# A drain of GpSimd between the scatters of the last wide item and the last block, in a fused attention and mixture-of-experts kernel

## The chip, the cores and the metric

The kernel runs on one core of a Trainium2 chip. The metric is the device time of one execution in microseconds (us), as a median over several runs. The profile is of one further execution.

## The reference

The reference computes a clustered attention and feeds its output, one row of 512 numbers per token, to a router with eight experts. Cut to what matters:

```python
# attention: 4 batches, 8 heads, 768 positions, head size 64, 16 clusters per head
mask = q_assign[:, :, :, None] == k_assign[:, :, None, :]     # nearest centroid of q and of k
scores = np.where(mask, scale * q @ k.T, -1e9)
attn = softmax(scores) @ v
x = attn.transpose(0, 2, 1, 3).reshape(3072, 512)

# router: 3072 tokens, 8 experts, hidden size 1024
expert_idx = argmax(cosine(x, expert_emb) / tau)
for e in range(8):
    mask = expert_idx == e
    out[mask] = gate_w[mask, None] * (np.maximum(x[mask] @ w1[e], 0) @ w2[e])
```

Every token goes to one expert alone, so the rows of x have to be gathered by expert, and the results scattered back to the rows of the output.

## The kernel before

The kernel has two phases. In the first (up to about 340 us) it works through 16 pairs of heads: TensorE makes the scores, ScalarE the exponentials, TensorE the product with v, and the finished rows go to a buffer x_rows in HBM. In the second, the tokens are sorted by expert, and the two matrix products of each expert are done in "items": four early blocks of 128 rows, then eight wide ("sized") items, one per expert, of 272 down to 160 rows, between single blocks of 128 rows. The list of kinds is at line 1314; it ends with a wide item and a block. The order of all instructions on all five engines is the order of the program's text (tc.manual_schedule, line 1404); no scheduler moves them, and each engine takes its own instructions in that order.

GpSimd issues all the indirect transfers of the second phase. gather (line 1038) fetches 128 rows, or quarter rows of 128 numbers, by an index per partition; scatter (line 1048) writes such rows to the output. A wide item's result is scattered by send (line 1238), one scatter for each 32 rows of it: nine for the widest, five for the last. A block's result (result, line 1268) is scaled by ScalarE with the gate and scattered at once by one scatter of 128 whole rows (line 1287). Both are recorded at line 1050. No engine waits for a scatter but to use its buffer anew, and at the end, where the output has to be complete.

The loop over the later items (line 1558) works one item ahead. For item i it does, in this order: the transposition of the next item's rows, the fetch of the one after it, send of the wide item before it (line 1570), the first matrix product of item i (hidden or sized_hidden), the loads of further weights, and the second product (result or sized_result). In the last round (i == LAST) item i is the last block: so its scatters on GpSimd are the five of the last wide item, from send at line 1570, and then the one of the block, from result. Two rounds from the end (line 1560) stands overflow(), a branch that does more blocks if an expert got more tokens than its places hold. In the profiled execution GpSimd skips it.

Behind the program's last statement (all instructions of it are recorded at the last line of the launch, L1634) each engine has a drain and then a barrier. An engine reports to GpSimd that it has come, and waits until GpSimd lets all go. SyncE first waits for every transfer to have landed. GpSimd has one drain before the barrier. After the barrier it clears the semaphores, with two more drains, and a second barrier ends the program. With the one at the program's start GpSimd has four drains.

Of the kernel before, what the change touches and what calls it, by code (L numbers as in the profile page):

```python
# [39 lines left out]
def kernel(  # L40
# [12 lines left out]
    nc = tc.nc  # L53
# [994 lines left out]
    def scatter(to, at, of, n):  # L1048

        inst = nc.gpsimd.indirect_dma_start(  # L1050
            out=to,
            out_offset=bass.IndirectOffsetOnAxis(ap=at, axis=0),
            in_=of,
            in_offset=None,
            bounds_check=n - 1,
            oob_is_err=False,
        ).ins
        tc.declare_no_dep(
            inst, group="out", reason="a row of out is written by one slot of one item"
        )  # L1060
        tc.add_to_no_dep_group("out", inst)
# [16 lines left out]
    def weights1(it, parts=1):  # L1078
        it.e = expert_of(it)
        for i in range(parts):  # L1080
            load_part(w1s[it.slot], moe_w1, it.e, KD, i, parts)

    def weights2(it, parts=1):
        for i in range(parts):
            load_part(w2s[it.slot], moe_w2, it.e, KF, i, parts)
# [7 lines left out]
    def fetch(it):  # L1093
        mo[it] = {}
        if it.kind == "sized":
            u0, n = FIRST[it.j], WIDE[it.j]
            xs = mo[it]["xs"] = szp.tile([P, max(WIDE), P], F32, tag="xs", name="xs")
            for u in range(n):
                gather(xs[:, u], x_pieces, flat(gpidx)[:, u0 + u : u0 + u + 1], NQ * N)
            return  # L1100
        if it.kind == "whole":
            xin = mo[it]["xin"] = it.xin
            gather(
                xin.rearrange("p w x -> p (w x)"), x_rows, it.tables[1][:, it.col : it.col + 1], N
            )
            return
        xin = mo[it]["xin"] = xip.tile([P, NQ, P], F32, tag="xin", name="xin")
        if it.kind == "early":
            n = SA * P
            gather(  # L1110
                xin.rearrange("p w x -> p (w x)"), x_rows[0:n], gidxs[0][:, it.j : it.j + 1], n
            )
            return
        for w in range(NQ):
            gather(xin[:, w], x_pieces, it.tables[0][:, it.col, w : w + 1], NQ * N)
# [11 lines left out]
    def turn_x(it, evict=None, xT=None):  # L1127
        d = mo[it]
        if it.kind == "sized":
            n = WIDE[it.j]  # L1130
            d["xT"] = szp.tile([P, KD, SQ * max(WIDE)], F32, tag="xTs", name="xTs")
            for u in range(0, n, NQ):
                m = min(NQ, n - u)
                nc.vector.transpose(
                    d["xT"][:, :, SQ * u : SQ * u + SQ * m].rearrange(
                        "p c (w t) -> p w c t", t=SQ
                    ),
                    d["xs"][:, u : u + m].rearrange("p w (c i) -> p w c i", i=SQ),
                )
            return  # L1140
        d["xT"] = mop.tile([P, DM], F32, tag="xTm", name="xTm") if xT is None else xT
        if it.kind == "block":
            nc.vector.transpose(
                d["xT"].rearrange("p (c w t) -> p w c t", c=KD, t=SQ),
                d["xin"].rearrange("p w (c i) -> p w c i", i=SQ),
            )
            return
        bk = psX.tile([P, DM], F32, tag="x_ps", name="x_ps")
        for c in range(KD):
            nc.tensor.transpose(  # L1150
                bk[:, P * c : P * c + P], d["rows"][:, c].rearrange("p w i -> p (w i)"), ident
            )
        evict(d["xT"], bk)

    def order_w2(it):

        w2 = mo[it]["w2"] = szp.tile([P, KF, DM], F32, tag="w2o", name="w2o", bufs=1)
        for f in range(KF):
            nc.vector.tensor_copy(
                w2[:, f].rearrange("p (g w i) -> p g w i", w=NQ, i=SQ),  # L1160
                w2s[it.slot][:, f].rearrange("p (w g i) -> p g w i", w=NQ, i=SQ),
            )
# [75 lines left out]
    def send(it):  # L1238

        u0 = FIRST[it.j]  # L1240
        for u in range(WIDE[it.j]):
            at = flat(spidx)[:, u0 + u : u0 + u + 1]
            scatter(out_pieces, at, mo[it]["ys"][:, u], NQ * N)
        del mo[it]

    def flat(t):
        return t.rearrange("p k w -> p (k w)")
# [156 lines left out]
    with tc.manual_schedule(engines=by_hand):  # L1404
# [118 lines left out]
        def overflow():  # L1523
            n_used = nc.values_load(used[0:1, 0:1], min_val=0, max_val=KX + NO)
            slot = later[-1].slot

            def more(j0, n):
                for j in range(j0, j0 + n):
                    it = Item("whole", KX + j, slot, more_tables)
                    it.col, it.gates, it.xin = j, more_gates, xin  # L1530
                    weights1(it)
                    weights2(it)
                    fetch(it)
                    order_x(it)
                    turn_x(it, nc.scalar.copy)
                    hidden(it)
                    result(it)

            with tc.If(n_used > KX):  # L1539
                more_tables = [None] + [  # L1540
                    mop.tile([P, NO], I32, tag=f"more{i}", name=f"more{i}", bufs=1)
                    for i in range(2)
                ]
                xin = szp.tile([P, max(WIDE), P], F32, tag="ys", name="ys")[:, 0:NQ]
                pb.hot_blocks(NB, NO)
                pb.tokens(NO)
                pb.token_rows(more_tables[1], more_tables[2])
                more_gates = mop.tile([P, NO], F32, tag="more_gates", name="more_gates", bufs=1)
                pb.hot_gates(NO)
                pb.gates(more_gates)  # L1550
                more(0, MORE[0])
                with tc.If(n_used > KX + MORE[0]):
                    more(MORE[0], MORE[1])
                    with tc.If(n_used > KX + MORE[0] + MORE[1]):
                        more(MORE[0] + MORE[1], MORE[2])

        LAST = len(later) - 1
        for i, it in enumerate(later):
            if i == LAST - 1:
                overflow()  # L1560
                weights1(later[LAST])
                weights2(later[LAST])
            if it.kind == "sized":
                order_w2(it)
            if i + 1 < len(later):
                turn_x(later[i + 1])
            if i > 0 and i + 2 < len(later) and later[i + 2].kind == "sized":
                fetch(later[i + 2])
            if i > 0 and later[i - 1].kind == "sized":
                send(later[i - 1])  # L1570
            if it.kind == "sized":
                sized_hidden(it)
            else:
                hidden(it)
            if i == 0:
                pb.gates(slot_gates)
            for j in range(i + 2, min(i + 4, len(later))):
                if later[j].kind == "block" and later[j] not in mo:
                    if it.kind == "sized":
                        nc.gpsimd.tensor_copy(pace, mo[it]["hT"][0:1, KF - 1, 0:1])  # L1580
                        fetch(later[j])
            if i + 2 < LAST:
                weights1(later[i + 2])
                if it.kind == "sized":
                    weights2(later[i + 2])
            if it.kind == "sized":
                sized_result(it)
            else:
                result(it)
            if i == 0:  # L1590
                fetch(later[2])
            if i + 2 < LAST and it.kind != "sized":
                weights2(later[i + 2])
# [45 lines left out]
```

## Time and profile before

| What | Value |
|---|---|
| Median of 6 runs | 712.4 us (710.99 to 713.04) |
| The profiled execution: its own time | 713.68 us |
| Its span, first to last instruction | 711.8 us |
| Busy share of the span: TensorE, VectorE, ScalarE, GpSimd | 98%, 54%, 38%, 38% |
| Granted TensorE clock, mean | 0.993 |
| Scatters of the output, from wide items and from blocks | 56 and 12 |
| Gathers | 96, of which 56 for wide items |
| Landing of a scatter of a wide item, median from its issue | 2.4 us |

The profile's page gives for each engine the busy time, then the chain of waits followed back from the last instruction, and the costliest groups of instructions. Register, branch and semaphore instructions and drains are not counted as busy; a q behind an engine's name (POOLq, SPq) marks the work of its sequencer, such as waits and drains. POOL is GpSimd, PE TensorE, DVE VectorE, ACT ScalarE, SP SyncE. In the timeline each line has the start and the length in us, then engine, line, operation, output and input, and in brackets the idle time before it and what ended it. The length of an indirect transfer's record is what GpSimd spends on it and not the time until its data has landed.

### The profile page before, as it was taken

How to read it: one execution, taken by the hardware profiler on the slowest of the kernel's cores; microseconds unless marked ns; L12 is line 12 of the kernel's file. 1: busy time of each engine (PE TensorE's matmuls, PEld its weight loads, DVE VectorE, ACT ScalarE, POOL GpSimd, SP SyncE). 2: the span in 40 equal slices, each digit the busy share in tenths (PEclk: the TensorE clock that was granted, in tenths of full speed). 3: DMA queues.
4: the chain of work that ended last, by engine and by line, in shares of the span. 5: the costliest groups of instructions: out<-in, count | busy, mean ns of one | idle time of the engine just before them, and what ended most of it. 6: DMA issues, size and time to landing. Idle time of an engine off the chain costs nothing.

```text
span 711.8 us, 16021 instructions
## 1 busy us (share of the span) xinstructions
PE 697.9 (98%) x6462; PEld 455.8 (64%) x6462; DVE 381.2 (54%) x665; ACT 268.4 (38%) x454; POOL 267.1 (38%) x402
## 2 busy tenths in 40 slices
PE   7999999999999999999999999999999999999995
PEld 3444444444444444444876668897979797979793
DVE  4588887998879999998675111330120303031210
ACT  4556565677556666567415110101011111111110
POOL 2122221432224212354042636736365454645412
PEclk9899999999999999999999999999999999999999
DMA  9446656676558687869799997268768686879450
GB/s 148 74 68 104 105 93 110 134 150 109 96 91 157 117 163 148 132 174 337 144 325 323 356 331 250 76 257 282 263 202 291 211 305 239 307 243 332 145 196 29
DMA packets 244123, 135.53 MB, mean 190 GB/s; under 512 B 207808, under 2 KB 207810, under 8 KB 244044
## 3 DMA queue, kind: packets, MB, share of 16 engines
q1 hardware_dynamic: 237852, 121.28, 64.0%
q0 software_dynamic: 6016, 13.12, 5.3%
q8 instruction: 53, 0.87, 0.5%
q14 instruction: 26, 0.21, 0.1%
q10 hardware_dynamic: 176, 0.05, 0.0%
HBM read 115.92 MB, written 13.12 MB: 181 GB/s over the span
## 4 chain that ended last, share of the span: by engine, by line
PE 84%; issue 5%; DMA 4%; DVE 4%; SPq 1%; POOL 1%; ACT 0%; POOLq 0%; DVEq 0%; ACTq 0%
PE s_ps L484 20%; PE o_ps L506 16%; PE h_ps L1259 10%; PE y_ps L1275 10%; PE h_ps L1174 9%; PE misc L1209 5%; PE y_ps L1209 5%; PE x_ps L1174 3%; DMA out_dram<-ys,spidx 3%; PE misc L553 2%; PE misc L396 2%; DVE acc L525 1%; PE misc L628 1%; DMA k<-in_k_dram 1%; POOL out_dram L1050 1%
## 5 line engine op out<-in xcount | busy, mean ns | idle before, releaser
L495 ACT ACTIVATE prob<-s_ps 128x768 f32<-128x768 f32 x192 | 153.6, 812 | 96.1 <-PE s_ps L484 75.5
L484 PE MATMUL s_ps<-qT,kT 64*64 64x384 f32 x1536 | 157.6, 486 | 0.0
L506 PE MATMUL o_ps<-prob,v 64*64 64x385 f32 x1536 | 143.6, 490 | 0.0
L525 DVE TENSOR_TENSOR acc<-acc,prob 128x768 f32<-128x768 f32 x128 | 124.9, 976 | 8.5 <-DVE acc L525 0.5
L506 PEld LDWEIGHTS o_ps<-prob,v 64*64 64x64 f32 x1536 | 54.6, 134 | 71.4 <-issue 60.0
L1259 PEld LDWEIGHTS h_ps<-xTm,w1s 128*128 128x128 f32 x768 | 87.4, 192 | 2.3 <-issue 1.6
L539 POOL TENSOR_TENSOR o_sum<-o_sb 128x385 f32<-128x385 f32 x30 | 32.2, 1072 | 150.3 <-ACT o_sb L530 150.3
L1218 DVE STREAM_TRANSPOSE ys<-y_ps 128x256 f32<-128x256 f32 (+4 forms) x16 | 6.7, 417 | 152.7 <-PE y_ps L1209 152.7
L1259 PE MATMUL h_ps<-xTm,w1s 128*128 128x128 f32 x768 | 88.3, 275 | 0.0
L1050 POOL DMA_INDIRECT out_dram<-ys,spidx x56 | 56.8, 1015 | 74.5 <-DVE ys L1234 59.5
L1275 PE MATMUL y_ps<-w2s,hT 128*128 128x512 f32 x192 | 84.5, 593 | 0.0
L484 PEld LDWEIGHTS s_ps<-qT,kT 64*64 64x64 f32 x1536 | 56.9, 134 | 38.1 <-issue 35.1
L1174 PE MATMUL h_ps<-xTs,w1s 128*128 128x272 f32 (+7 forms) x384 | 72.9, 346 | 0.8 <-ACTq L1539 0.8
L1174 PEld LDWEIGHTS h_ps<-xTs,w1s 128*128 128x128 f32 x384 | 66.6, 190 | 8.1 <-issue 2.9
L1266 ACT ACTIVATE hT<-h_ps 128x512 f32<-128x512 f32 x24 | 14.3, 596 | 143.7 <-PE h_ps L1259 143.7
L484 PE MATMUL s_ps<-hot 64*64 64x384 bf16 x768 | 65.7, 329 | 2.2 <-ACT prob L495 1.2
L574 POOL COPY inv<-inv 32x12 f32<-32x12 f32 x120 | 44.6, 372 | 55.0 <-DVE inv L571 50.6
L1039 POOL DMA_INDIRECT xs<-x_rows,gpidx x56 | 57.3, 1023 | 17.1 <-issue 16.8
L1275 PEld LDWEIGHTS y_ps<-w2s,hT 128*128 128x128 f32 x192 | 35.6, 190 | 40.2 <-issue 40.2
L484 PEld LDWEIGHTS <-hot 64*64 64x64 bf16 x768 | 24.0, 107 | 40.0 <-issue 38.3
L1209 PE MATMUL misc<-hTs,w2o 128*128 128x272 f32 (+7 forms) x256 | 48.0, 346 | 0.0
L1209 PE MATMUL y_ps<-hTs,w2o 128*128 128x272 f32 (+7 forms) x256 | 48.0, 346 | 0.0
(264 smaller groups left out, 688.9 us busy)
## 6 DMA issues: line engine op xcount, KB each, us to landing
w1s<-in_moe_w_dram SPq DMA_DIRECT2D x18, 2048.0 KB, 11.1
w2s<-in_moe_w_dram SPq DMA_DIRECT2D x18, 2048.0 KB, 14.4
v<-in_v_dram SPq DMA_DIRECT2D x128, 48.0 KB, 2.1
q<-in_q_dram SPq DMA_DIRECT2D x60, 96.0 KB, 3.6
k<-in_k_dram SPq DMA_DIRECT2D x60, 96.0 KB, 3.7
x_rows<-xb SPq DMA_DIRECT2D x60, 96.0 KB, 2.8
xr<-x_rows SPq DMA_DIRECT2D x9, 512.0 KB, 4.1
w1s<-in_moe_w_dram SPq DMA_DIRECT2D x4, 1024.0 KB, 10.0
```

Source lines behind the costliest of these rows:

```text
L484: nc.tensor.matmul(s_ps[D * half : D * half + D, h, 0:HS], lhsT=l[rows, half], rhs=r[rows], start=part == (1 if len(parts) < 2 else 0), st ...
L495: nc.scalar.activation(d["prob"][:, :, 0:HS], d["s_ps"][:, :, 0:HS], ACTF.Exp, scale=scale)
L506: nc.tensor.matmul(g["o_ps"][D * h : D * h + D, half, 0:HE], lhsT=ld[n]["v"][keys, j, h], rhs=d["prob"][keys, h, 0:HE], start=(j == 0), st ...
L525: nc.vector.tensor_tensor(g["acc"], g["acc"], d["prob"][:, :, 0:HS], ALU.add)
L539: add(t["o_sum"][:, hq], t["o_sb"][:, 0], t["o_sb"][:, 1], ALU.add)
L574: nc.gpsimd.tensor_copy(inv2[M * to : M * to + M, :, i % 2], inv[M * i : M * i + M])
L1039: nc.gpsimd.indirect_dma_start(out=to, out_offset=None, in_=of, in_offset=bass.IndirectOffsetOnAxis(ap=at, axis=0), bounds_check=n - 1, oo ...
L1050: inst = nc.gpsimd.indirect_dma_start(out=to, out_offset=bass.IndirectOffsetOnAxis(ap=at, axis=0), in_=of, in_offset=None, bounds_check=n - 1,
L1174: nc.tensor.matmul(bk, lhsT=w1s[it.slot][:, c, P * f : P * f + P], rhs=d["xT"][:, c, 0:C], start=(c == 0), stop=(c == KD - 1),)
L1209: nc.tensor.matmul(bks[g][:, 0:C], lhsT=d["w2"][:, f, P * g : P * g + P], rhs=d["hT"][:, f, 0:C], start=(f == 0), stop=(f == KF - 1),)
L1259: nc.tensor.matmul(bk[:, m : m + P], lhsT=w1s[it.slot][:, c, f0 + m : f0 + m + P], rhs=d["xT"][:, P * c : P * c + P], start=(c == 0), stop ...
L1275: nc.tensor.matmul(bk, lhsT=d["hT"][:, P * c : P * c + P], rhs=w2s[it.slot][:, c], start=(c == 0), stop=(c == KF - 1),)
```

## The change

In the last round of the loop over the later items, GpSimd gets one more drain, behind the five scatters of the last wide item and ahead of the scatter of the last block. A drain lets an engine go on to its next instruction when what it has under way is done. The drain waits for no semaphore and sets none.

```diff
@@ -1568,6 +1568,8 @@
                 fetch(later[i + 2])
             if i > 0 and later[i - 1].kind == "sized":
                 send(later[i - 1])
+                if i == LAST:
+                    nc.gpsimd.drain()
             if it.kind == "sized":
                 sized_hidden(it)
             else:
```

The lines behind it move by two: the new drain is at L1572, and the program's end at L1636.

## The prediction

> **What bounds the kernel now.** I read the page's chain of waits first, because the change adds one instruction to one engine and touches no data. By lines, the chain is TensorE work almost everywhere; GpSimd appears only at its end.
>
> ```profile
> PE 84%; issue 5%; DMA 4%; DVE 4%; SPq 1%; POOL 1%; ACT 0%; POOLq 0%; DVEq 0%; ACTq 0%
> ```
>
> The reader should see that an instruction on GpSimd can only matter where TensorE has stopped. So the next view is the timeline of GpSimd in the last 22 us, where the five scatters of the last wide item and the scatter of the last block stand.
>
> ```profile
> 691.63 0.97 POOL L1050 DMA_INDIRECT out_dram<-ys,spidx  x1 [18.02 <-DVE ys L1234]
> ...
> 696.74 0.97 POOL L1050 DMA_INDIRECT out_dram<-ys,spidx  x1 [0.30 <-issue]
> 705.12 0.97 POOL L1050 DMA_INDIRECT out_dram<-y,sidx  x1 [7.41 <-ACT y L1286]
> ```
>
> GpSimd is free from 696.74 + 0.97 = 697.71 to about 704.9. In that stretch TensorE computes the last block's result, and ScalarE then scales it (start 704.16, 0.69 long, so y is ready at 704.85). The scatter at 705.12 is the last work of the kernel; its record ends at 706.09, yet the span ends at 711.8. Those 5.7 us are a tail with no compute, so I asked for the instructions of the program's closing line, cut at 710.92, and for who waits on SyncE.
>
> ```profile
> L1634 SPq EVENT_SEMAPHORE  x11: 27/28/25962, 681.8 to 708.4; - x11
> L1634 SPq DRAIN  x2: 7/10/13, 708.4 to 708.5; - x2
> L1634 PEldq DRAIN  x1: 6212/6212/6212, 698.0 to 698.0; - x1
> L1634 ACTq DRAIN  x1: 717/717/717, 704.2 to 704.2; - x1
> L1634 POOLq DRAIN  x1: 6017/6017/6017, 704.9 to 704.9; - x1
> ```
>
> The columns are instruction count, shortest/median/longest time in ns, and first and last start. At the end every engine drains and then meets at a barrier. SyncE has first waited for the last scatter to land (its wait ends at 681.8 + 26.0 = 707.8), has gone through ten short waits and is done at 708.5. TensorE's drain ends at 698.0 + 6.2 = 704.2, with its last matmul; ScalarE's at 704.9. GpSimd's own drain starts at 704.89, when the last scatter is handed out, lasts 6.02 and ends at 710.9. It is the last to arrive: it holds the barrier 2.4 us longer than SyncE. What follows takes 0.9:
>
> ```profile
> L1634 POOLq EVENT_SEMAPHORE  x4: 17/17/17, 710.9 to 711.7; - x4
> L1634 POOLq DRAIN  x2: 40/76/113, 711.1 to 711.5; - x2
> ```
>
> So the end of this kernel is set by a drain of GpSimd, and drains of the same engine with nothing newly queued took 0.04 and 0.11 us.
>
> **The change, part by part.** It removes nothing and moves nothing: in the order of the instructions all five engines have the rows that they had, with one drain more on GpSimd, between the fifth scatter of the last wide item (696.74) and the scatter of the last block (705.12). No other engine waits for it by a semaphore. Queued behind it on GpSimd are only the last scatter with its register move and its wait, and then the closing drain. Who waits for these: SyncE for the scatter's landing, everybody for the barrier.
>
> Cost of the new drain in its place. I split the closing drain: it starts at 704.89, the scatter ahead of it ends at 706.09, so 1.20 of it is that scatter and 6.02 - 1.20 = 4.82 is something after it. This something is not GpSimd being busy with the scatter: scatters follow each other every 1.28 us (start to start), so about 0.31 after a record's end the engine takes the next. It is not only the landing either: that is over at 707.8, and the drain goes on 3.1 us. Laid behind the fifth scatter, the same 4.82 runs from 697.71 to 702.5. Lower bound: 0.04 to 0.19 (drains with no scatter ahead, at the start and the end). Middle: the landing of the fifth scatter, 2.2 after its start, about 698.9. Upper bound: 4.82 for each scatter not yet landed when the drain begins; the fourth and fifth are (landing takes 2.2 to 3.2), so 9.6, to 707.3. I take 4.82, the nearest row. Its cover is the wait for y until 704.85: 7.14 us long, 2.3 more than needed. Without that cover it would cost its whole 4.82, since the last scatter stands behind it.
>
> What it saves. The value in dispute is what the closing drain still costs when an earlier drain has been run and only one scatter has come since. If the 4.82 is work piled up by all the indirect transfers since the start (the page counts 56 + 56 + 32 + 12 + 4 + 4 = 164, so 29 ns each), the early drain does nearly all of it beside TensorE, and the closing one has one scatter's share: it ends about 706.4, or with the landing, 707.8. Next late is then SyncE at 708.5. The barrier opens 710.9 - 708.5 = 2.4 earlier; the 0.9 behind it stays. If it is a fixed price that any drain behind a scatter pays, the closing drain stays 6.02 and nothing is saved.
>
> Two pages of the Trainium skill speak against a gain. "VectorE: DVE Perf Modes", section "The DRAIN you can't avoid", calls the drains of a program's head and tail a constant of some 12 ns on all engines; by it there would be nothing to move and the change is worth 0.0. The row of 6017 ns contradicts it: here the drain is the last event of the tail. "PSUM — Partial Sum Buffer", section "Engine vs sequencer instructions", says that a drain waits for its engine to go fully idle. By that, the closing drain should end 0.3 after the scatter's record, at 706.4, and not 4.5 later; an early drain would end at 698.0 and leave nothing. It fits TensorE's 6212 ns drain (which ends with the matmuls), but leaves most of GpSimd's row open. I follow the row: there is work beyond the engine's visible instructions.
>
> Sum against the profiled execution: span 711.8 - 2.4 = 709.4. That execution took 713.7, so 1.9 lies around the span, and it would take 711.3. It stands 1.3 above the median of the six runs (712.4), so I take the difference from the median: 712.4 - 2.4 = 710.0.
>
> **The rivals.**
> First, the forecast: the early drain takes the piled-up work, the closing one is short, SyncE ends last. 710.0. For it: a drain at the start and two after the barrier, with nothing new queued, take 0.04 to 0.19, so the price depends on what came since the last drain, and there was none since the start. Against it: no row shows a drain behind a single scatter.
>
> Second, a fixed price: 4.82 is paid behind any scatter, however few. Then the early drain is hidden between 697.71 and 702.5 and the closing one is as long as now: 712.4. For it: a drain that must ask all 16 DMA engines whether they are done would cost the same for one transfer as for 164. A mixed price (part of it fixed) lies between this and the first; up to 1.4 of gain it counts as no change.
>
> Third, slower: the early drain outlasts its cover and holds back the last scatter. It decides from 7.14 us of drain behind the fifth scatter. At the upper bound, 9.6, it ends at 707.3, the last scatter goes out 2.4 later than at 704.9, and its landing, the closing drain (again 4.82 behind one scatter) and the barrier move by 2.4: 712.4 + 2.4 = 714.8. For it: the closing drain has one scatter fresh and takes 4.82; the early one has two still in flight. Against it: DMA is nearly empty there (the five scatters landed 2.2 to 3.2 after their start), so a wait on flight ends near 699. To this case I count a smaller one, in which the first scatter behind a drain is itself dearer.
>
> That the drain does nothing at all (the closing drain's length is set by its own scatter alone) gives 712.4 too and is in the second.
>
> **How the numbers follow.** A measurement of this kernel can tell about 0.2% from no change, 1.4 us: faster is below 711.0, slower above 713.8. The first case gets 0.52, the second with the mixed price 0.28, the third 0.20. The first case's own range is 709.2 to 710.9 (the runs of before spread from 711.0 to 713.0 about their median, and a partly fixed price would leave some 0.5 to 1.0 of the gain away). For 8 times in 10 the second must be in, and most of the third: 709.2 to 714.9. Left out are a dearer early drain and a gain above 3.2, which the tail could not give before SyncE's end is moved.
>
> **What would show it.** Right: a drain record at the new line, starting about 696.5 (when the fifth scatter is handed out, 0.23 ahead of its record as with the last one) and some 6 long, ending before 704; the last scatter still 0.27 behind ScalarE's y; the closing drain under 3.6 us; SyncE's last drain before the barrier within 0.1 of GpSimd's arrival; a span near 709.4. If the closing drain is 6.0 again, the second case holds. If the last scatter starts more than 0.5 behind y, the third. The prediction would be wrong from its base if the early drain's record were under 0.5: then the 4.82 belongs to the program's end and not to a drain behind scatters.

## The result and the profile after

The changed kernel takes 709.8 us (median of 19 runs, 708.5 to 711.5), the kernel before 712.2 (40 runs): the ratio is 0.9969, with a 95% interval of 0.9960 to 0.9977. That is 2.2 us faster (1.6 to 2.8). 710.0 was forecast.

GpSimd's timeline in the changed kernel, in the stretch that was shown of the kernel before:

```profile
689.21 0.97 POOL L1050 DMA_INDIRECT out_dram<-ys,spidx  x1 [18.03 <-DVE ys L1234]
...
694.32 0.97 POOL L1050 DMA_INDIRECT out_dram<-ys,spidx  x1 [0.30 <-issue]
702.70 0.97 POOL L1050 DMA_INDIRECT out_dram<-y,sidx  x1 [7.41 <-ACT y L1286]
```

The idle time ahead of the last scatter is 7.41, as before, and it still ends with ScalarE's y. The new drain has held nothing back. The new line and the closing drain, in the view of a line's instructions (count, shortest/median/longest ns, first and last start), the closing one cut at 706.1:

```profile
L1572 POOLq DRAIN  x1: 8895/8895/8895, 691.1 to 691.1; - x1
```

```profile
L1636 SPq EVENT_SEMAPHORE  x11: 28/28/25875, 679.5 to 705.9; - x11
L1636 SPq DRAIN  x2: 7/10/13, 706.0 to 706.1; - x2
L1636 PEldq DRAIN  x1: 6212/6212/6212, 695.5 to 695.5; - x1
L1636 ACTq DRAIN  x1: 717/717/717, 701.7 to 701.7; - x1
L1636 POOLq DRAIN  x1: 2952/2952/2952, 702.5 to 702.5; - x1
```

The closing drain fell from 6.02 to 2.95. It ends at 702.47 + 2.95 = 705.42, 0.08 behind the landing of the last scatter (705.34, where SyncE's long wait of 25.875 ends), and SyncE, done at 706.1, is now the last to reach the barrier. From the end of ScalarE's y to the end of the span it was 711.81 - 704.85 = 6.96; it is 706.98 - 702.42 = 4.56. This stretch is called the tail from here on. It has lost 2.4.

The spans differ by more, 711.8 against 707.0. The other 2.42 lie ahead of y, and arose at the start: the first 30 us, in the view by stages, first of the kernel before, then of the changed one (after the busy times come the granted clock, the DMA share and GB/s):

```profile
0.00:30.00 30.00, 25.28 (x210) 11.59 (x214) 15.15 (x44) 13.37 (x26) 4.14 (x23) 0.89 0.79 108
```

```profile
0.00:30.00 30.00, 24.28 (x242) 11.45 (x246) 17.46 (x46) 15.85 (x31) 5.10 (x24) 1.00 0.83 111
```

The granted clock was 0.89 there in one and 1.00 in the other execution, and the one with the full clock got through 242 matmuls instead of 210. It is the same code, and both kernels' runs spread over some 3 us. So the spans of two profiles can't be compared whole here; the tail can, as it starts from y.

### The profile page after: what moved, and what is told of

The parts are those of the page before. It is cut to its first block, busy times and chain, and to the rows that moved or that the text cites. A ratio compares the mean times of both kernels' runs of the same rounds, so it can differ in the third digit from the quotient of the medians.

```text
span 707.0 us, 16022 instructions
## 1 busy us (share of the span) xinstructions
PE 694.5 (98%) x6462; PEld 454.5 (64%) x6462; DVE 381.4 (54%) x665; ACT 268.5 (38%) x454; POOL 265.7 (38%) x402
## 4 chain that ended last, share of the span: by engine, by line
PE 84%; DVE 5%; issue 5%; DMA 4%; POOL 1%; POOLq 0%; ACT 0%; SPq 0%; DVEq 0%; ACTq 0%
PE s_ps L484 19%; PE o_ps L506 16%; PE h_ps L1259 10%; PE y_ps L1275 10%; PE h_ps L1174 9%; PE y_ps L1209 5%; PE misc L1209 5%; PE x_ps L1174 3%; DMA out_dram<-ys,spidx 3%; PE misc L553 2%; DVE acc L525 2%; PE misc L396 2%; PE misc L628 1%; DMA k<-in_k_dram 1%; PE misc L641 0%
```

## The experiments

Each gives a time against the kernel before on the same chip, and a trace. Differences of time in the text are worked out from the ratio. Three quantities are used. n is the count of indirect transfers between a drain and the drain ahead of it (or the start). The "overhang" is the time from the end of the last transfer's record to the drain's end. The landing is the last update of a transfer's semaphore, and is counted from the same record's end: 1.66 for the last scatter of the kernel, 4.6 to 6.6 behind the last transfer ahead of a drain in the middle of the second phase, where the weights load. From e5 on the runs were on two further chips, where the kernel before took 719.5 to 721.2 and its runs spread over 5 to 7 us; the tail tells more there than the median. The tail of the kernel before, 6.96, is that of its one trace, from the first chip.

**e1: the drain ahead of all indirect transfers.**

```diff
-        (3, 2, 3): lambda: [fetch(it) for it in E0[0:3]],
+        (3, 2, 3): lambda: [nc.gpsimd.drain()] + [fetch(it) for it in E0[0:3]],
```

> The new drain stands ahead of the first of the 164 indirect transfers, and nowhere else. Theory A (each indirect transfer since the last drain leaves some 20 ns of work, 3.1 in all, which a drain does behind the landing): the new drain is short, under 1.5, the closing one is as in the kernel before, 6.0, of which 3.1 behind the landing, and the time is that of before within 1 us. Theory B (a drain has a price paid once in a program, whatever came before it): the new one takes some 3, the closing one 2.95 as in the changed kernel, and the time falls by 2.4. If what piles up is GpSimd's arithmetic, of which most lies ahead of this place, the closing drain falls too, by half or more.

Measured: 712.1 against 712.6, ratio 0.9989 (0.9978 to 1.0001); tail 6.97.

```profile
L1307 POOLq DRAIN  x1: 1299/1299/1299, 313.5 to 313.5; - x1
...
L1634 POOLq DRAIN  x3: 40/113/6020, 704.0 to 710.6; - x3
```

The new drain ends 0.06 behind an addition on GpSimd that was still running, so it had next to nothing to do itself. The closing drain (the longest of the three at L1634) is as long as before. So theory B falls: a drain has no price that is paid once. GpSimd's arithmetic does not count either, as most of it (90 of 106 us) stood ahead of this drain. What the closing drain pays for came with the indirect transfers.

**e2: the drain at half of them.**

```diff
                         fetch(later[j])
+                        if i == 4:
+                            nc.gpsimd.drain()
```

> The new drain stands at about half of the indirect transfers: 79 ahead of it, 85 behind. Theory A: the new one ends some 1.5 behind the landing of what stands ahead of it, the closing one 85 x 19 ns = 1.6 behind the landing, some 4.5 long, and the time falls by about 1.5. Theory B: 3.1 and 0.1 behind the landing, the closing one 2.95 long, and the time falls by 2.4. A third theory, C (only the last transfers matter, say those of the last rounds): the closing one stays 6.0 and the time does not move.

Measured: 714.7 against 712.6, ratio 1.0027 (1.0015 to 1.0039), slower by 1.9. The lines of the new and of the closing drain:

```profile
L1583 POOLq DRAIN  x1: 12122/12122/12122, 502.1 to 502.1; - x1
...
L1636 POOLq DRAIN  x3: 46/113/8215, 702.4 to 711.2; - x3
```

No theory had this. A drain that had taken 79 of 164 transfers out of the pile made the closing one longer, 8.2 instead of 6.0. The tail is 9.16, 2.2 more, as the time says. Theory A as first put, 19 ns for each of 164, is wrong.

**e3: six drains, in every second round.** The edit is that of e2 with `if i > 1:`.

> Six drains, one behind each block's gathers in rounds 2 to 12, so with 59, 20, 20, 18, 18 and 16 indirect transfers since the drain before, and 13 ahead of the closing one. Theory A: the first ends 1.1 behind its landing, the others 0.3 to 0.4, the closing one 0.25: 3.1 to 3.2 long. Theory B: the first 3.1, all others 0.1. The time falls by 2.0 to 2.4 by either, unless the drains that wait for gathers under full DMA load hold back the scatters behind them; that costs nothing while the buffers of results suffice.

Measured: 708.9 against 712.6, ratio 0.9946 (0.9929 to 0.9964); tail 4.56, as in the changed kernel.

```profile
L1583 POOLq DRAIN  x6: 9599/9686/11158, 461.6 to 648.3; - x6
...
L1636 POOLq DRAIN  x3: 46/113/3442, 702.6 to 706.8; - x3
```

The six drains end 2.46, 0.86, 0.85, 0.77, 0.77 and 0.69 behind their landings, with n of 59, 20, 20, 18, 18 and 16, and the closing one 0.57 with n = 13. That is 41 to 43 ns for each, so the work goes by the count, and each drain starts it anew; theory B had 0.1 for all but the first. The size, though, is twice the 19 ns. The six runs are 1.4 us faster than the tail explains. This goes with the granted clock: five of the six had a mean of 0.998, and took 708.9. Of the 29 runs of before, nine come near that, with 0.996 or 0.997, and took 711.2; the other 20 had 0.995 or less. Against those nine the gain is 2.3, that of the tail.

**e4: the drain without its cover.**

```diff
+                if it is later[-1]:
+                    nc.gpsimd.tensor_copy(pace, y[0:1, 0:1])
+                    nc.gpsimd.drain()
                 scatter(out[:], to, y, N)
```

> A copy of one number from the last block's scaled result and behind it the drain, both ahead of the last scatter: the drain cannot begin before the result is ready, so nothing covers it. The five scatters have landed by then, so the drain has only the piled-up work. Theory A or B: copy 0.2, drain 3.1 to 3.3, so the last scatter starts 3.3 to 3.6 later than in the kernel before; the closing drain saves 2.4 of it: 0.9 to 1.2 slower than before, 3.3 to 3.6 slower than the changed kernel. If the 3.1 is a wait that starts with the last scatter's end, whoever waits, the drain is over at once and the time falls by 2.2.

Measured: 714.6 against 712.6, ratio 1.0032 (1.0019 to 1.0045), slower by 2.3; tail 10.07.

```profile
705.40 0.18 POOL L1288 COPY pace<-y 1x1 f32<-1x1 f32 x1 [7.27 <-ACT y L1286]
711.12 0.98 POOL L1050 DMA_INDIRECT out_dram<-y,sidx  x1 [5.54 <-issue]
...
L1289 POOLq DRAIN  x1: 4938/4938/4938, 705.4 to 705.4; - x1
```

The second column of the first two lines is the length, the bracket the idle time ahead. The drain ends at 705.39 + 4.94 = 710.33, so 4.75 behind the copy's end, and not 3.1 to 3.3: with every transfer long landed, it takes as long as when it has a landing to wait for. So a good part of the work had run beside the landing in the kernel before. And so a drain without cover costs its whole length: the last scatter starts 5.85 behind y instead of 0.27, so 5.58 later; some 2.5 of that comes back behind it, and the tail is 3.1 longer. The measured 2.3 has that just inside its interval (1.4 to 3.2).

**e5 to e8: the drain at four other places.** The edit is that of e2 with i = 2, 6, 8 and 10.

> One new drain with 59 indirect transfers ahead and 105 behind. The runs so far put a drain at 1.7 behind its last transfer's record plus 0.043 for each transfer since the last drain, up to 79 of them, but 3.1 for 163 or 164 without a drain and 5.3 for 85 behind a drain. Theory A2 (43 ns each, and without a drain the pile is cut to some 72 at one point): the closing drain ends 1.7 + 4.5 = 6.2 behind the last scatter's record, 1.4 later than before; slower by about 1.4. Theory D (the price goes by the place in a ring, not by the count): it may be anything from 1.7 to 7, and no line through 0, 13 and 65 fits it. Theory A as first put (19 ns each): 3.7, faster by 1.1.

> 99 ahead, 65 behind. Theory A2: the closing drain ends 1.7 + 2.8 = 4.5 behind the last scatter's record, 0.3 sooner than before. Theory A as first put: 2.9, 1.9 sooner. Theory D: off that line.

> 117 ahead, 47 behind. Theory A2: 1.7 + 2.0 = 3.7 behind the last scatter's record, 1.1 sooner than before. Theory A as first put: 2.6, 2.2 sooner. Theory D: off that line.

> 135 ahead, 29 behind. Theory A2: 1.7 + 1.2 = 2.9 behind the last scatter's record, 1.9 sooner than before. Theory A as first put: 2.3, and SyncE sets the end: 2.4 sooner. Theory D: off that line.

Measured: e5 726.4 against 720.6, ratio 1.0072 (1.0049 to 1.0095), tail 10.79; e6 725.4, 1.0062 (1.0035 to 1.0089), tail 7.53; e7 720.0, 0.9988 (0.9962 to 1.0014), tail 6.05; e8 717.8, 0.9951 (0.9924 to 0.9978), tail 5.03. The closing drain in e5, the longest of all, in the view cut to the stretch from 685 to 719, and then the new drain and the closing one of e7 and of e8:

```profile
L1636 POOLq DRAIN  x2: 113/4982/9850, 708.9 to 719.0; - x2
```

```profile
L1583 POOLq DRAIN  x1: 9296/9296/9296, 587.7 to 587.7; - x1
...
L1636 POOLq DRAIN  x3: 46/113/5113, 710.6 to 716.3; - x3
```

```profile
L1583 POOLq DRAIN  x1: 9823/9823/9823, 622.7 to 622.7; - x1
...
L1636 POOLq DRAIN  x3: 46/113/4093, 710.9 to 715.6; - x3
```

Overhangs of the closing drains, with those of the others:

| Kernel | n of the closing drain | Overhang | Behind the landing |
|---|---|---|---|
| after | 1 | 1.75 | 0.08 |
| e3 | 13 | 2.24 | 0.57 |
| e8 | 29 | 2.89 | 1.23 |
| e7 | 47 | 3.91 | 2.24 |
| e6 | 65 | 5.38 | 3.72 |
| e2 | 85 | 7.01 | 5.34 |
| e5 | 105 | 8.64 | 6.98 |
| before | 164 | 4.81 | 3.15 |

From 47 to 105 each transfer adds 82 ns, from 1 to 29 it adds 41 (A2 had 41 throughout, and falls). The bend lies where 41 ns x n passes the landing, 1.66 (n = 40). All rows but the last then follow one rule: overhang = max(41 ns x n, landing) + 41 ns x n. I read it as work in two halves: one runs beside the landing, the other only when both are over. Worked out, the rows give 1.70, 2.19, 2.85, 3.85, 5.33, 6.97 and 8.61: within 0.06. The new drains in the middle fit as well, each with its own landing: e5 with n = 59 and a landing of 5.01 has 5.01 + 2.42 = 7.43 against 7.47, e6 with n = 99 and a landing of 6.56 has 6.56 + 4.06 = 10.62 against 10.65.

The kernel before does not fit with 164, which would give 13.4. Its 4.81 fits n = 59, which gives 4.84. The new drains of e7 and e8, with no drain ahead, show the same: at 117 and 135 transfers they end 0.50 and 1.23 behind the landing, which is n = 12 and 30. All three are short by 105. So without a drain, the pile was cut at some place in the program, by its first 105. The traces show a pause of GpSimd that goes with it, ahead of the 114th transfer, first in the kernel before, then in e2:

```profile
582.26 1.04 POOL L1039 DMA_INDIRECT xin<-x_rows,gpidx  x1 [3.13 <-issue]
```

```profile
577.24 1.04 POOL L1039 DMA_INDIRECT xin<-x_rows,gpidx  x1 [0.54 <-issue]
```

GpSimd stands idle for 3.13 there instead of 0.54, with nothing in the profile that it waits for. It does so in the eight traces in which no drain had been run between the first and the 113th transfer, and in none of the six with such a drain. So the cut is most likely made at this place, where it takes 2.6 us of GpSimd and leaves 113 - 105 = 8 transfers in the pile. That the pause is the cut is argued from their standing together; what sets it off is not shown. The missing cut is why e2 and e5 are slower than no drain: their drain at 79 or 59 kept the pile from growing to where it is cut, and left 85 or 105 for the end instead of 59.

e6 lost more (4.5) than its tail (0.57). Its drain stood until 565.6, and in its trace the round behind it, from one block's scaled result to the next, took 39.4 instead of 36.5. TensorE waited once in it, which it does not do there in the kernel before:

```profile
PE x_ps L1174 <- ACT hTs L1181: 2.6, 1, 2.6
```

Whether the drain brought this wait about is not shown. e5 lost and e8 gained some 1.5 more than their tails; both tails lie inside the intervals.

**e9 and e10: without the overflow branch.** Left out is overflow(), which computes nothing for these inputs. e9 is the kernel before without it, e10 is e2 without it.

```diff
             if i == LAST - 1:
-                overflow()
```

> The kernel before without the branch for experts with too many tokens (left out: it computes nothing for these inputs, but GpSimd passes it by with waits and one bookkeeping instruction, 1.23 long, between transfers 158 and 159). The closing drain's pile so far: 41 ns for each transfer up to 99, then 12 transfers' worth at 117 and 30 at 135 (as if cut to nothing at 105), and 76 at 164 where 59 would be expected. If the branch's bookkeeping doubles the older part, the closing drain now ends 59 x 41 ns = 2.4 behind the landing instead of 3.15. If not, 3.15 again. Theory A as first put (all 164 at 19 ns) has 3.15 too. The time may fall by some us, as SyncE and TensorE pass no branch; that is no part of the question.

> The drain with 79 transfers ahead and 85 behind, and without that branch (left out as said of the run before). With it the closing drain ended 5.34 behind the landing, for 85 transfers. If the branch's bookkeeping doubles the older part: now 85 x 41 ns = 3.5. If the doubling has another cause: 5.3.

Measured: e9 720.3 against 721.2, ratio 0.9981 (0.9959 to 1.0003), closing drain 6.02 long and 3.16 behind the landing; e10 722.0, ratio 1.0014 (0.9993 to 1.0035), closing drain 8.21 and 5.34 behind. No drain has moved; the tails are 6.87 and 9.06, and in the times no difference can be told. The branch has no part in it, and it needs none, since the two halves explain the doubling.

**e11: a drain ahead of the five scatters, and one without cover that has only five.** The edit is that of e4 and this:

```diff
+                if i == LAST:
+                    nc.gpsimd.drain()
                 send(later[i - 1])
```

> Two new drains: one ahead of the five scatters of the last wide item, and one behind a copy of one number of the last block's result and ahead of its scatter, when the five scatters have long landed. The first takes the pile of 158, some 3 to 4 us, beside TensorE's work. The second has five transfers, landed: if a drain's 1.7 behind a transfer is a wait for the landing alone, it ends 5 x 41 ns = 0.2 behind the copy; if the 1.7 is a price of its own, 1.9. The closing drain has one transfer: 2.95. The time against before: by the landing alone, copy and drain hold back the last scatter by 0.7, 1.7 faster; by a price of its own, by 2.4, about the same as before.

Measured: 720.0 against 721.2, ratio 0.9985 (0.9963 to 1.0006): no difference that can be told; tail 5.81 instead of 6.96.

```profile
L1289 POOLq DRAIN  x1: 681/681/681, 714.9 to 714.9; - x1
...
L1574 POOLq DRAIN  x1: 4313/4313/4313, 691.2 to 691.2; - x1
```

Neither drain had a transfer in flight. The second (L1289; its record includes the 0.18 of the copy) ends 0.48 behind the copy, and 2 x 41 ns x 5 is 0.41: the 1.7 in an overhang is the landing and no price of its own. The first takes 4.31, and 2 x 41 ns x (158 - 105) is 4.35. So the two halves run one behind the other when no landing is awaited, and at 158 transfers the cut has been made. The gain is less than forecast for this case (1.7), since copy, drain and restart hold the last scatter back by 1.3 and not 0.7.

**e12: the drain at the 106th transfer.** The edit is the change itself with `if i == 7:`.

> One new drain with 106 indirect transfers ahead and 58 behind: the line of the changed kernel, but six items earlier. The eleven runs so far fit one rule, E: a drain ends max(41 ns x n, landing) + 41 ns x n behind the record of the last transfer, with n the transfers since the last drain, less 105 once there are more than 105. By it the new drain has n = 1 and ends within 0.1 of the landing of its last scatter, and the closing one has n = 58 and ends 4.76 behind the last scatter's record, as in the kernel before (59: 4.81): no change of the time, within 0.2%. Without the cut at 105 the new drain has n = 106 and ends 8.7 behind its last scatter's record, the next scatter starts late, and the closing one is the same.

Measured: 718.9 against 719.5, ratio 0.9999 (0.9978 to 1.0021), tail 6.96.

```profile
L1572 POOLq DRAIN  x1: 14979/14979/14979, 561.0 to 561.0; - x1
...
L1636 POOLq DRAIN  x3: 46/113/6008, 709.4 to 716.0; - x3
```

The time is as rule E had it, and the closing drain's overhang too (4.80). The new drain's is not: 9.00, where the rule with its landing of 4.62 gives 8.97 for n = 106 and 4.7 for n = 1. So at 106 the pile was still whole, and at 117 (e7) it was cut by 105. This fits the pause ahead of the 114th transfer, which is missing here as in all kernels with an earlier drain. The cut takes the first 105 transfers.

## Why the prediction was right, step by step

**The bound.** The step "it is the last to arrive: it holds the barrier 2.4 us longer than SyncE" was right, and is the gain: SyncE now sets the end, and the tail is shorter by 2.4. The reading "GpSimd appears only at its end" was not: in order of time the chain of waits runs along GpSimd and its transfers from 648 on. The step did not rest on that, as it was read from the closing line. That the median met 710.0 within 0.2 is in part chance, with runs that spread over some 3 us.

**The early drain in its place.** I took the nearest row, 4.82 behind the fifth scatter; it was 4.73 (695.29 to 700.03). The row could be carried over because both drains met nearly the same pile. It ended 2.4 ahead of y, where 2.3 was forecast to be spare. Wrong was where its record would begin: 3.2 ahead of the fifth scatter (691.1, where three scatters were still to be started) instead of 0.23 ahead of it. I had read the closing drain's start as the rule, but that drain stood behind a scatter that waited for y. So the new record is 8.9 and not 6.0 long, at no cost.

**What the closing drain has left.** Between "about 706.4, or with the landing, 707.8" it was the landing: 1.75 behind the record, with 0.08 behind the landing. Either is ahead of SyncE.

**The size of the work.** This step failed: "29 ns each" for 164 transfers. It is 82 ns (two halves of 41) for 59 of them. The 29 ns were worked back from the 4.82, so that they give it again proves nothing; 4.82 was right since I had it from the row as a whole. A sum from 29 ns would have failed at other places, as e2 and e5 show: there the forecast's own logic, less pile and thus a shorter end, has the wrong sign.

**The rivals.** The fixed price is out by the closing drain of the changed kernel, 0.08 behind its landing, and by e11, where a drain with five landed transfers took under 0.5. The third, an early drain that outlasts its cover, did not come about in the change; e4 shows its price, 5.6 on the last scatter and 3.1 on the tail. Its upper bound, 4.82 for each scatter in flight, was the wrong unit: what is in flight costs its landing and no more.

**The two pages.** In the Trainium skill, "PSUM — Partial Sum Buffer", section "Engine vs sequencer instructions", has a drain wait for its engine to go idle. That is too little here: in e11 GpSimd had run no transfer and no computation for 7.8 us, only waits and one bookkeeping instruction, all transfers had landed, and the drain still took 4.31. "VectorE: DVE Perf Modes", section "The DRAIN you can't avoid", with its constant of 12 ns is nearer to the drains behind the barrier (46 and 113 ns), and far from the one ahead of it in both kernels (6017 and 2952).

**The sum.** The difference was taken from the median and not from the span, and that was needed: the two profiled executions differ by 2.4 in their first 30 us.

## What to carry to other kernels

If a kernel ends with a drain that is longer than its engine's last work, look at what that drain has to clear, and clear it earlier, under cover. On GpSimd it was here some 82 ns for each indirect transfer since the last drain, so the early drain belongs behind nearly all of them and where the engine has to wait anyhow for at least that long. Do not put it in the middle by reasoning that less is left: with 85 or 105 transfers behind it, it made this kernel slower than with none. Several drains on the way do as well as one late one, as long as the last stands near the end: e3 has six, with 13 transfers behind the last, and has the tail of the changed kernel.

## What the runs showed of the hardware that was not expected

- A drain of GpSimd behind n indirect transfers ends max(41 ns x n, landing) + 41 ns x n after the last one's record. With nothing in flight it is the two halves alone. All drains behind transfers in the fourteen traces agree within 0.1, with 105 taken off where the pile had been cut. The 41 ns and the 105 are read from these same traces; of drains forecast by the whole rule there are the two of e12, where the closing one fits and the new one showed that the cut comes later. Every transfer here has 128 rows, so whether the price goes by the transfer or by the row can't be told, nor what the work is.
- Without an earlier drain the pile was cut once, by 105, most likely in a pause of 2.6 us of GpSimd ahead of the 114th transfer, which the same kernels show and no others. Whether it is cut again later, none of the kernels could show: they have 164.
- A drain's record can begin while transfers ahead of it are still to be started (691.1 with starts at 691.8, 693.0 and 694.3), so its length alone says little; its end does.
